# Two rounds of first loads, and the projections of 256 rows ahead of the last two transposes, in a fused SwiGLU feed-forward kernel

## The chip, the cores and the metric

The kernel runs on one core of a Trainium2 chip. The metric is device time in microseconds of one execution; the time before is the median of five runs. One more execution was recorded by the hardware profiler, and all times inside the kernel come from that record.

## The reference

The input x has 2048 rows of 640 columns in bf16 (a leading dimension of 1 is left out here); w_gate and w_up are 640 x 1536, w_down is 1536 x 640.

```python
def reference(x, w_gate, w_up, w_down):
    g = _silu(x @ w_gate)
    u = x @ w_up
    return (g * u) @ w_down
```

## The kernel before

**Tiling.** The rows of x are cut into four blocks of 512 (`sb`), each block into four pieces of 128 rows (`SUB` is 4). The 640 columns are five slices of 128 (`KD`, index `kd`), the 1536 hidden columns are twelve slices of 128 (`KF`, index `fc`). All weights and the whole transposed input `xT` stay in SBUF (the on-chip memory, 128 partitions wide).

**The main loop.** For each block and each `fc`, `proj` issues five matmuls that add up 128 hidden columns x 512 rows of the gate product in a PSUM tile `pg`, and five more for the up product in `pu` (line 133). ScalarE computes Silu of `pg` into `sg` (L170), VectorE multiplies it with `pu` into `aT` (L171). After the twelve `fc` of a block, for each piece of 128 rows, 24 matmuls compute the output (`po_a` of 512 columns at L180, `po_b` of 128 columns at L189), ScalarE copies the result to SBUF, and SyncE (SP) sends it out.

**The start.** TensorE needs x transposed. For the blocks 1 to 3 a transposing DMA does that (L96). For block 0 the four pieces of x are loaded as they are into `x_sb` and TensorE transposes them: `transpose_chunk(c, ...)` issues five transposes (L124) of piece `c` into a PSUM tile `pt`, and a copy takes that to `xT` (L129). The copies are VectorE's, but for three of the five slices of the last piece, which ScalarE takes. Pieces are transposed in the order 0, 2, 1, 3. Ahead of them `warm(N_WARM)` issues 20 matmuls on a tile of ones (L102), which compute nothing that is used, and two more stand between the last transpose and the first projection. The first gate projection is split by rows: 0 to 383, then 384 to 511; the up projection covers all 512.

**The loads.** The first loads go out on two DMA queues, SP's and ScalarE's, each in the order of the code: SP loads the x pieces 0 and 1, ScalarE the pieces 2 and 3 (L73); then both load the first 128 columns of w_gate (SP three of the five slices, ScalarE two), then those of w_up (L86). All further weight chunks go out on SP (L70), gate and up in turn: columns 128 to 383 first, then three chunks of 384 columns each. The framework gives the DMAs eight semaphores in turn, so that the ninth DMA must wait until the DMA that had the first semaphore has landed, the tenth until that of the second has, and so on.

**The order of the work.** The framework orders each engine's instructions and sets the waits. `keep_order`, called at the end of the first step (`sb == 0`, `fc == 0`), holds TensorE and ScalarE to the order in which the code names the instructions. TensorE works in order: an instruction that waits holds up all that stand behind it.

Of the kernel before, what the change touches and what calls it, by code (L numbers as in the profile page):

```python
# [10 lines left out]
def _body(  # L11
# [8 lines left out]
    nc = tc.nc  # L20
    P = nc.NUM_PARTITIONS
# [5 lines left out]
    B, S0, D = x.shape  # L27
    F = w_gate.shape[1]
    S = B * S0
# [3 lines left out]
    KD = D // P  # L33
    KF = F // P
    S_BLK = 512
    NSB = S // S_BLK
    SUB = S_BLK // P
    DA = 512
    N_WARM = 20
    W_CHUNKS = [(0, 1), (1, 3), (3, 6), (6, 9), (9, 12)]  # L40
    assert D % P == 0 and F % P == 0 and S % S_BLK == 0 and D > DA and SUB >= 2

    consts = ctx.enter_context(tc.tile_pool(name="consts", bufs=1))
    work = ctx.enter_context(tc.tile_pool(name="work", bufs=3))
# [8 lines left out]
    wg_sb = consts.tile([P, KD, F], bf16)  # L53
    wu_sb = consts.tile([P, KD, F], bf16)
# [7 lines left out]
    wg_v = w_gate.rearrange("(kd p) f -> p kd f", p=P)  # L62
    wu_v = w_up.rearrange("(kd p) f -> p kd f", p=P)
    wd_v = w_down.rearrange("(kf p) d -> p kf d", p=P)

    def wslice(a, b):
        return slice(a * P, b * P)
# [4 lines left out]
    def load_x(eng, c0, c1):  # L72
        eng.dma_start(out=x_sb[:, c0:c1, :], in_=x_v[:, c0:c1, :])  # L73
# [4 lines left out]

    queues = (nc.sync, nc.scalar)
    halves = ((0, KD // 2 + 1), (KD // 2 + 1, KD))  # L80
    for c in (0, 1):
        for i, eng in enumerate(queues):
            load_x(eng, c + 2 * i, c + 2 * i + 1)
    for dst, src in ((wg_sb, wg_v), (wu_sb, wu_v)):
        for eng, (k0, k1) in zip(queues, halves):
            eng.dma_start(out=dst[:, k0:k1, wslice(0, 1)], in_=src[:, k0:k1, wslice(0, 1)])  # L86
    load_w(nc.sync, wg_sb, wg_v, *W_CHUNKS[1])
# [12 lines left out]
    def warm(n):  # L100
        for _ in range(n):
            nc.tensor.matmul(  # L102
                pw[:, 0:P], lhsT=ones[:], rhs=ones[:], start=True, stop=True
            )

    def keep_order(engine):

        traced = [i for i in nc.cur_bb.bb.instructions if i.engine == engine]
        for a, b in zip(traced, traced[1:]):
            tc.add_manual_dep(  # L110
                b,
                a.name,
                mybir.DependencyInfo(
                    mybir.DependencyClass.NoSync, mybir.DependencyReason.DATA
                ),
                reason="keep_order",
            )

    def transpose_chunk(c, parts):
        c_sl = slice(c * P, (c + 1) * P)  # L120
        for copy, tag, k0, k1 in parts:
            pt = psum.tile([P, k1 - k0, P], bf16, tag=tag, name="pt")
            for kd in range(k0, k1):
                nc.tensor.transpose(  # L124
                    out=pt[:, kd - k0, :],
                    in_=x_sb[:, c, kd * P : (kd + 1) * P],
                    identity=ident[:],
                )
            copy(out=xT[:, k0:k1, c_sl], in_=pt[:])  # L129

    def proj(ps, w_sb, fc, sb, c0, c1):
        for kd in range(KD):
            nc.tensor.matmul(  # L133
                ps[:, c0:c1],
                lhsT=w_sb[:, kd, fc * P : (fc + 1) * P],
                rhs=xT[:, kd, sb * S_BLK + c0 : sb * S_BLK + c1],
                start=(kd == 0),
                stop=(kd == KD - 1),
            )

    for sb in range(NSB):
        s_sl = slice(sb * S_BLK, (sb + 1) * S_BLK)
        for fc in range(KF):
            pg = psum.tile([P, S_BLK], f32, tag="gu", name="pg", bufs=4)
            pu = psum.tile([P, S_BLK], f32, tag="gu", name="pu", bufs=4)
            if sb == 0 and fc == 0:
                h = (SUB - 1) * P
                warm(N_WARM)
                for n, c in enumerate((0, 2, 1)):
                    transpose_chunk(  # L150
                        c, [(nc.vector.tensor_copy, ("po_a", "po_b")[n % 2], 0, KD)]
                    )
                transpose_chunk(
                    SUB - 1,
                    [
                        (nc.vector.tensor_copy, "po_b", 0, 2),
                        (nc.scalar.copy, "po_a", 2, KD),
                    ],
                )
                warm(2)  # L160
                proj(pg, wg_sb, fc, sb, 0, h)
                proj(pg, wg_sb, fc, sb, h, S_BLK)
                proj(pu, wu_sb, fc, sb, 0, S_BLK)
                keep_order(mybir.EngineType.PE)
                keep_order(mybir.EngineType.Activation)
            else:
                proj(pg, wg_sb, fc, sb, 0, S_BLK)
                proj(pu, wu_sb, fc, sb, 0, S_BLK)
            sg = work.tile([P, S_BLK], f32)
            nc.scalar.activation(sg[:], pg[:], ACT.Silu)  # L170
            nc.vector.tensor_tensor(  # L171
                out=aT[:, fc, s_sl], in0=sg[:], in1=pu[:], op=ALU.mult
            )

        for j in range(SUB):
            s0 = sb * S_BLK + j * P
            last = sb == NSB - 1 and j == SUB - 1
            po_a = psum.tile([P, DA], f32, tag="po_a", name="po_a")
            for kf in range(KF):
                nc.tensor.matmul(  # L180
                    po_a[:],
                    lhsT=aT[:, kf, s0 : s0 + P],
                    rhs=wd_sb[:, kf, 0:DA],
                    start=(kf == 0),
                    stop=(kf == KF - 1),
                )
            po_b = psum.tile([P, D - DA], f32, tag="po_b", name="po_b")
            for kf in range(KF):
                nc.tensor.matmul(  # L189
                    po_b[:],  # L190
                    lhsT=aT[:, kf, s0 : s0 + P],
                    rhs=wd_sb[:, kf, DA:D],
                    start=(kf == 0),
                    stop=(kf == KF - 1),
                )
            ot = outp.tile([P, D], bf16)
            nc.scalar.copy(ot[:, 0:DA], po_a[:])  # L197
            if not last:
                nc.scalar.copy(ot[:, DA:D], po_b[:])  # L199
                nc.sync.dma_start(out=out2[s0 : s0 + P, :], in_=ot[:])  # L200
            else:
                nc.sync.dma_start(out=out2[s0 : s0 + P, 0:DA], in_=ot[:, 0:DA])
                nc.vector.tensor_copy(out=ot[:, DA:D], in_=po_b[:])  # L203
                nc.scalar.dma_start(out=out2[s0 : s0 + P, DA:D], in_=ot[:, DA:D])
# [76 lines left out]
def kernel(tc, *args):  # L281
    _body(tc, *args)
    tc.close()
    tc.compile()
    _trim(tc.nc)
# [30 lines left out]
```

## Time and profile before

| | |
|---|---|
| median of five runs | 164.85 us (164.42 to 165.17) |
| profiled execution, its own time | 164.42 us |
| its span, first to last instruction | 163.1 us |
| TensorE busy | 159.3 us, 98% of the span |
| VectorE, ScalarE busy | 34.9 us, 44.0 us |
| DMA | 11.27 MB, nearly all loads in the first fifth of the span |

The profiled execution is the fastest of those shown, and 0.43 us below the median. Its span is 1.3 us shorter than its time; the rest lies around the first and the last instruction. In the profile PE is TensorE's matmuls and PEld its weight loads, which overlap with matmuls; DVE is VectorE, ACT is ScalarE, SPq and ACTq are the issuing of DMAs by SP and ScalarE. A row of a group or of the timeline names the line, the operation, output and input tile, shape and count. The chain of waits is followed back from the last instruction, at each step to whatever released it.

### The profile page before, as it was taken

What the parts mean: (1) busy time and instruction counts of PE and PEld (TensorE: products, weight loads), DVE (VectorE), ACT (ScalarE), POOL (GpSimd) and SP (SyncE); (2) the same over time, 40 slices, a digit from 0 to 9 for tenths busy, and PEclk for the clock granted to TensorE, in tenths of its full rate; (3) what the DMA queues carried; (4) which work ended last, traced back from release to release, by engine and by line L of the source; (5) the groups of instructions that cost most, each with busy time, mean ns of one, the idle gap of its engine ahead of it and who ended that gap; (6) DMA issues with size and microseconds to landing.
All of it is one profiled execution on the core that took longest, in us unless ns stands there. A gap on an engine that the chain in (4) does not pass through costs nothing.

```text
span 163.1 us, 2121 instructions
## 1 busy us (share of the span) xinstructions
PE 159.3 (98%) x894; PEld 80.4 (49%) x911; DVE 34.9 (21%) x54; ACT 44.0 (27%) x82; POOL 0.6 (0%) x6
## 2 busy tenths in 40 slices
PE   9899999999999999999999999999999999999994
PEld 8444444456544444455554444445554444445552
DVE  2322233300022333310002333330001333331000
ACT  3222222123322222222232222222233222222321
POOL 1000000000000000000000000000000000000000
PEclk9999999999999999999999999999999999999999
DMA  7999999911110000001210000001111000000112
GB/s 224 261 334 331 362 202 221 159 40 44 40 40 0 0 4 0 0 2 40 81 43 0 0 2 0 0 4 40 40 40 40 4 0 0 0 0 0 44 47 74
DMA packets 18953, 11.27 MB, mean 69 GB/s; under 512 B 9728, under 2 KB 18944, under 8 KB 18944
## 3 DMA queue, kind: packets, MB, share of 16 engines
q1 hardware_dynamic: 17968, 10.65, 24.1%
q10 hardware_dynamic: 976, 0.49, 1.0%
q8 instruction: 7, 0.11, 0.3%
q14 instruction: 2, 0.02, 0.0%
HBM read 6.55 MB, written 2.62 MB: 56 GB/s over the span
## 4 chain that ended last, share of the span: by engine, by line
PE 94%; DMA 4%; issue 1%; DVE 0%; DVEq 0%
PE pg L133 31%; PE pu L133 31%; PE po_a L180 25%; PE po_b L189 7%; DMA wg_sb<-in_w_gate_dram 3%; DMA x_sb<-in_x_dram 2%; DVE ot L203 0%; DVEq L203 0%
## 5 line engine op out<-in xcount | busy, mean ns | idle before, releaser
L133 PE MATMUL pg<-xT,wg_sb 128*128 128x512 bf16 (+2 forms) x242 | 59.5, 375 | 0.6 <-DMA wg_sb<-in_w_gate_dram 0.3
L133 PE MATMUL pu<-xT,wu_sb 128*128 128x512 bf16 x233 | 59.1, 379 | 0.4
L171 DVE TENSOR_TENSOR aT<-sg,pu 128x512 bf16<-128x512 f32 x48 | 33.0, 687 | 111.0 <-PE pu L133 111.0
L170 ACT ACTIVATE sg<-pg 128x512 f32<-128x512 f32 x48 | 28.7, 597 | 72.7 <-PE pg L133 72.7
L180 PE MATMUL po_a<-wd_sb,aT 128*128 128x512 bf16 x185 | 43.4, 379 | 0.3
L133 PEld LDWEIGHTS <-wg_sb 128*128 128x128 bf16 x245 | 23.6, 98 | 28.2 <-DMA wg_sb<-in_w_gate_dram 1.1
L133 PEld LDWEIGHTS <-wu_sb 128*128 128x128 bf16 x240 | 23.4, 98 | 28.1 <-DMA wu_sb<-in_w_up_dram 0.3
L180 PEld LDWEIGHTS <-aT 128*128 128x128 bf16 x192 | 18.3, 98 | 19.8
L197 ACT CAST ot<-po_a 128x512 bf16<-128x512 f32 x16 | 9.4, 585 | 40.4 <-PE po_a L180 38.0
L189 PEld LDWEIGHTS <-aT 128*128 128x128 bf16 x192 | 12.1, 98 | 3.8
L189 PE MATMUL po_b<-wd_sb,aT 128*128 128x128 bf16 x192 | 13.3, 219 | 0.1
L199 ACT CAST ot<-po_b 128x128 bf16<-128x128 f32 x15 | 4.0, 265 | 1.1
L102 PE MATMUL pw<-ones 128*128 128x128 bf16 x22 | 2.6, 305 | 0.4 <-DVE ones L77 0.4
L203 DVE CAST ot<-po_b 128x128 bf16<-128x128 f32 x1 | 0.3, 291 | 12.3 <-PE po_b L189 12.3
L102 PEld LDWEIGHTS <-ones 128*128 128x128 bf16 x22 | 2.2, 142 | 0.4 <-DVE ones L77 0.4
L129 DVE COPY xT<-pt 128x640 bf16<-128x640 bf16 (+1 forms) x4 | 1.5, 436 | 2.9 <-PE pt L124 2.9
L124 PE MATMUL pt<-ident,x_sb 128*128 128x128 bf16 x20 | 1.8, 255 | 0.0
L88 ACT ACT_TABLE_LOAD x1 | 1.3, 1283 | 2.0 <-issue 2.0
L124 PEld LDWEIGHTS <-x_sb 128*128 128x128 bf16 x20 | 1.6, 121 | 0.2 <-DMA x_sb<-in_x_dram 0.2
L129 ACT COPY xT<-pt 128x384 bf16<-128x384 bf16 x1 | 0.5, 478 | 0.8 <-PE pt L124 0.8
masks.py:199 POOL TENSOR_SCALAR_AFFINE_SELECT ident<-ident 128x128 bf16<-128x128 bf16 x1 | 0.3, 292 | 0.1
L88 ACT ACTIVATE silu_first<-ones 128x1 f32<-128x1 bf16 x1 | 0.2, 202 | 0.0
(6 smaller groups left out, 0.8 us busy)
## 6 DMA issues: line engine op xcount, KB each, us to landing
out_dram<-ot SPq DMA_DIRECT2D x15, 160.0 KB, 1.8
wd_sb<-in_w_down_dram SPq DMA_DIRECT2D x1, 1920.0 KB, 12.6
wg_sb<-in_w_gate_dram SPq DMA_DIRECT2D x3, 480.0 KB, 7.8
wu_sb<-in_w_up_dram SPq DMA_DIRECT2D x3, 480.0 KB, 7.5
x_sb<-in_x_dram SPq DMA_DIRECT2D x2, 160.0 KB, 2.7
x_sb<-in_x_dram ACTq DMA_DIRECT2D x2, 160.0 KB, 2.9
wg_sb<-in_w_gate_dram SPq DMA_DIRECT2D x1, 320.0 KB, 4.4
wu_sb<-in_w_up_dram SPq DMA_DIRECT2D x1, 320.0 KB, 5.0
```

Source lines behind the costliest of these rows:

```text
L88: nc.scalar.activation(silu_first[:], ones[:, 0:1], ACT.Silu)
L102: nc.tensor.matmul(pw[:, 0:P], lhsT=ones[:], rhs=ones[:], start=True, stop=True)
L124: nc.tensor.transpose(out=pt[:, kd - k0, :], in_=x_sb[:, c, kd * P : (kd + 1) * P], identity=ident[:],)
L129: copy(out=xT[:, k0:k1, c_sl], in_=pt[:])
L133: nc.tensor.matmul(ps[:, c0:c1], lhsT=w_sb[:, kd, fc * P : (fc + 1) * P], rhs=xT[:, kd, sb * S_BLK + c0 : sb * S_BLK + c1], start=(kd == 0 ...
L170: nc.scalar.activation(sg[:], pg[:], ACT.Silu)
L171: nc.vector.tensor_tensor(out=aT[:, fc, s_sl], in0=sg[:], in1=pu[:], op=ALU.mult)
L180: nc.tensor.matmul(po_a[:], lhsT=aT[:, kf, s0 : s0 + P], rhs=wd_sb[:, kf, 0:DA], start=(kf == 0), stop=(kf == KF - 1),)
L189: nc.tensor.matmul(po_b[:], lhsT=aT[:, kf, s0 : s0 + P], rhs=wd_sb[:, kf, DA:D], start=(kf == 0), stop=(kf == KF - 1),)
L197: nc.scalar.copy(ot[:, 0:DA], po_a[:])
L199: nc.scalar.copy(ot[:, DA:D], po_b[:])
L203: nc.vector.tensor_copy(out=ot[:, DA:D], in_=po_b[:])
```

## The change

The eight first loads go out in another order. Each queue now has an x piece, its part of the gate columns, an x piece, its part of the up columns. SP has the pieces 0 and 2, ScalarE the pieces 1 and 3.

TensorE's order becomes: 17 warm matmuls; transposes of the pieces 0 and 1; two warm matmuls; the gate projection of rows 0 to 127, then of rows 128 to 255; transposes of the pieces 2 and 3; the up projection of rows 0 to 255; the gate projection of rows 256 to 511; the up projection of rows 256 to 511. The copies are shared out as before.

```diff
-    N_WARM = 20
+    N_WARM = 17
+    N_GAP = 2
...
-    for c in (0, 1):
+    for c, dst, src in ((0, wg_sb, wg_v), (SUB // 2, wu_sb, wu_v)):
         for i, eng in enumerate(queues):
-            load_x(eng, c + 2 * i, c + 2 * i + 1)
-    for dst, src in ((wg_sb, wg_v), (wu_sb, wu_v)):
+            load_x(eng, c + i, c + i + 1)
         for eng, (k0, k1) in zip(queues, halves):
             eng.dma_start(out=dst[:, k0:k1, wslice(0, 1)], in_=src[:, k0:k1, wslice(0, 1)])
...
-                h = (SUB - 1) * P
+                h = SUB // 2 * P
+                dve, act = nc.vector.tensor_copy, nc.scalar.copy
                 warm(N_WARM)
-                for n, c in enumerate((0, 2, 1)):
-                    transpose_chunk(
-                        c, [(nc.vector.tensor_copy, ("po_a", "po_b")[n % 2], 0, KD)]
-                    )
-                transpose_chunk(
-                    SUB - 1,
-                    [
-                        (nc.vector.tensor_copy, "po_b", 0, 2),
-                        (nc.scalar.copy, "po_a", 2, KD),
-                    ],
-                )
-                warm(2)
-                proj(pg, wg_sb, fc, sb, 0, h)
+                transpose_chunk(0, [(dve, "po_a", 0, KD)])
+                transpose_chunk(1, [(dve, "po_b", 0, KD)])
+                warm(N_GAP)
+                proj(pg, wg_sb, fc, sb, 0, P)
+                proj(pg, wg_sb, fc, sb, P, h)
+                transpose_chunk(2, [(dve, "po_a", 0, KD)])
+                transpose_chunk(3, [(dve, "po_b", 0, 2), (act, "po_a", 2, KD)])
+                proj(pu, wu_sb, fc, sb, 0, h)
                 proj(pg, wg_sb, fc, sb, h, S_BLK)
-                proj(pu, wu_sb, fc, sb, 0, S_BLK)
+                proj(pu, wu_sb, fc, sb, h, S_BLK)
```

## Prediction

> **What bounds the kernel now.** I read the page's head first, then the chain of waits over the first 9 us, then the timeline of that stretch, then what the SP queue waits for. The page says that TensorE is the kernel:
>
> ```profile
> span 163.1 us, 2121 instructions
> PE 159.3 (98%) x894; PEld 80.4 (49%) x911; DVE 34.9 (21%) x54; ACT 44.0 (27%) x82; POOL 0.6 (0%) x6
> ```
>
> PE is busy for 98% of the span, and the change leaves everything from the second pair of projections (fc=1) on as it is. So only the moment counts at which PE begins fc=1 and then runs without holes. The chain of waits, cut at 9 us, shows what sets it:
>
> ```profile
> 0.12 2.63 DMA x_sb<-in_x_dram
> 2.77 4.43 DMA wg_sb<-in_w_gate_dram
> 7.24 1.25 PE pg L133 x5
> 8.50 0.65 PE pu L133 x3
> ```
>
> (start, length, what). The chain before 7.24 holds no PE instruction: an x piece that lands at 2.75, a gate chunk (wg_sb columns 128 to 383) that SP issues at 2.77 and that lands at 7.20, then the matmuls of fc=1. The list of SP's own waits has one line that explains the 2.77:
>
> ```profile
> SPq L70 <- DMA x_sb<-in_x_dram: 0.9, 1, 0.9
> ```
>
> SP's first load at L70, the ninth of the program, waits for an x piece, and the chain's 0.12 names it: the first piece on ScalarE's queue (its issues are at 0.1 and 0.6). Last the timeline from 2.3 to 7.3 us (start, length, engine, line, operation; in brackets the idle time before and its releaser):
>
> ```profile
> 2.39 1.05 PEld L124 LDWEIGHTS <-x_sb 128*128 128x128 bf16 x10
> 3.27 1.51 DVE L129 COPY xT<-pt 128x640 bf16<-128x640 bf16 x4 [2.94 <-PE pt L124]
> 3.60 0.56 PEld L124 LDWEIGHTS <-x_sb 128*128 128x128 bf16 x10 [0.17 <-DMA x_sb<-in_x_dram]
> 4.38 0.48 ACT L129 COPY xT<-pt 128x384 bf16<-128x384 bf16 x1 [0.84 <-PE pt L124]
> 4.59 1.13 PEld L133 LDWEIGHTS <-wg_sb 128*128 128x128 bf16 x10 [0.31 <-DMA wg_sb<-in_w_gate_dram]
> 4.64 1.25 PE L133 MATMUL pg<-xT,wg_sb 128*128 128x384 bf16 x10 [0.19 <-DVE xT L129]
> 5.94 1.03 PE L133 MATMUL pu<-xT,wu_sb 128*128 128x512 bf16 x4
> 7.24 0.39 PE L133 MATMUL pg<-xT,wg_sb 128*128 128x512 bf16 x1 [0.27 <-DMA wg_sb<-in_w_gate_dram]
> ```
>
> Three readings. First, ten 128-column operations take 1.05 us before 3.4 and 0.56 us after it: PE's pace doubles there, from 0.105 to 0.056 us each (the windows print a granted clock of 1.00 on both sides, so I go by the paces). Second, pg's matmuls start at 4.64, when the third copy ends and the gate columns have just landed. Third, of pu's five matmuls one record is missing: at the 0.216 us of a 512-column matmul (1.08 for five) the first began at 5.73 and PE was free at 5.73 + 1.08 = 6.81. It then idles 0.43 us for the gate chunk. PE has slack there; the load does not. The next up chunk is as tight: issued at 3.18, 5.0 us to landing, so 8.2, against PE's 7.24 + 1.08 = 8.32.
>
> **The change part by part.** *The loads.* Same eight transfers, same bytes, two queues, four each; only the second and third on each queue change places. Landings, from issue plus time to landing: first x pair 2.3 and 2.75; second x pair 0.5 + 3.1 = 3.6 and 0.6 + 3.2 = 3.8; gate 0.91 + 3.6 = 4.5 and 1.03 + 3.7 = 4.7; up 1.38 + 3.9 = 5.3 and 1.52 + 3.8 = 5.3. What lands third in the new order completes the same bytes as before, so x pieces 2 and 3 at 4.5 and 4.7, and up at 5.3. Gate lands one x pair (1.1 us) earlier at about 3.5; its bounds are 3.1 (0.7 after the first pair, the gap that the up pair shows) and 4.7 (no earlier than now).
>
> *The ninth load.* The first piece on ScalarE's queue is still an x piece issued at 0.1, so SP goes on at 2.77, and the bytes ahead of the gate chunk are the same: 7.20. If the transfers mix better or worse I allow 0.3 either way, about half the spread between the third and the fourth pair; I take 0.
>
> *Warm-up.* Three matmuls fewer are 3 x 0.105 = 0.3 us; they end at 2.2 instead of 2.5. The first transpose waits for its x piece (2.35), so at most 0.1 us comes of it.
>
> *Transposes and projections.* PE executes in order, so I follow it. Transposes of pieces 0 and 1 (10 x 0.105): 2.4 to 3.45, the second piece being there at 2.75. Two warm matmuls: 3.6. The copies keep their places: first 3.27 to 3.75, second to 4.16. Gate columns at 3.5. So pg rows 0 to 127 run 3.8 to 4.1 (5 x 0.056) and rows 128 to 255 run 4.2 to 4.5 after the second copy. Then PE reaches the transposes of piece 2 and has that new wait in front of everything: 4.54 to 4.82, piece 3 to 5.10. VectorE starts a copy 0.27 us after the last transpose starts (4.11 to 4.38 in the ACT row): piece 2's 5.03 to 5.5, piece 3's first part to 5.8 (0.28), ScalarE's part 5.31 to 5.79 (0.48). PE meanwhile waits for the up columns at 5.3 (0.2 us idle), does pu rows 0 to 255 (5 x 0.109, midway between the 128- and the 512-column pace) to 5.85, pg's second half to 6.39, pu's second half to 6.94. So PE is free at 6.94 instead of 6.81. The earlier projections have gained nothing, because the up columns end the wait, and they come last in both orders; what they cost, 0.13 us, is covered by the gate chunk that lands at 7.20. That cover is worth 0.3 us. With gate at 4.7 the same walk ends at 7.6: 0.36 us late. With gate at 3.1 it is still 6.94. I take 6.94.
>
> *Copies, Silu, evictions.* ScalarE's Silu of fc=0 moves from 5.93 to about 6.7; the buffer that it frees is wanted by the third gate projection at 9.41. Nothing waits.
>
> *Sum.* fc=1 begins at 7.24 as before, the up chunk at 8.2 still fits, the 155.9 us that follow are unchanged: span 163.1 us, and the profiled execution 164.42 us (1.3 us around the span). The median of the five runs is 164.85, 0.43 above the profiled one. What fits that spread (0.75 us) is the moment at which PE's pace doubles: each us later costs half a us of PE's work once the slack of 0.43 is gone. With the slow pace to the end of fc=0, PE would be free at about 9.15 before and at 9.05 after (the 0.1 us of the warm-up). So 0 in the runs that the load bounds, -0.1 in those that PE bounds: 164.8.
>
> The page "TensorE: Matmul & The Clock Gate" of the Trainium skill (Part 1) says that the faster clock comes after a busy window of about 3.4 us whose phase runs free of the kernel. The trace has the change 3.0 us after the first matmul (0.39), which doesn't contradict it. The rule speaks against this change: it removes warm-up and puts four holes into that window. By it a window that is missed would cost 3.4 us at half pace, an estimate of up to 1.4 us; by the rows alone I count nothing. "DMA: Bandwidth & Descriptors" (Issuing engines are not separate DMA queues) has both queues interleave on the same 16 engines; the landings in pairs agree, and by it too reordering the queues can't move the last of the eight.
>
> **The rivals.** *No change (my forecast)*: own range 164.5 to 165.2, from the 0.3 us on the gate chunk either way.
>
> *Slower: the holes in PE's work delay the doubling of its pace.* PE now idles 0.2 us before the first transpose, about 0.2 and 0.1 between warm-up and the two pg parts, 0.2 for up; before it has 0.17 and 0.3. Against it: before, the pace doubled in spite of 0.4 us of idleness at the start and 0.17 at the very moment. Price: t us later cost t/2 minus the slack of 0.3; it decides from 0.6 us on. One more wait as long as the first (3.0 us) means 1.2 us at most: 166.0, typically half of that, 165.5. A late gate or up landing (the 0.36 above) would end at 165.2, on the edge of being seen.
>
> *Faster: the loads gain from mixing 256-byte rows of weights with 1280-byte rows of x*, and the gate chunk and the up chunk both land early. For it: the windows show 340 GB/s at 2.4 to 3.4, when x moves, and 193 GB/s from 4.64 to 5.73, so there is room. Against it: that slow stretch belongs to the chunks' own first packets, and SP's issue doesn't move. The bound is PE at 6.94, so 0.3 us, plus the 0.43 by which the median lies above the profiled run if that came from late x pieces, which the new order bears better: 0.3 to 0.7, 164.1 to 164.5.
>
> **How the numbers follow.** No change 0.48, slower 0.29, faster 0.23. A comparison of this kernel can tell about 0.3%, 0.5 us. Most of the forecast's own range lies within that (0.43 of the 0.48, the rest split), most of the slower rival's beyond it (0.27), of the faster one about as well (0.2, its bound being so near): faster 0.22, same 0.48, slower 0.30. The range for 8 in 10 takes in all of the faster rival and the slower one's typical price: 164.1 to 165.8.
>
> **What would show it.** Right: pg of fc=1 at 7.2 to 7.3, released by the gate chunk; SP's first L70 load at about 2.8; PE free by 7.0; an idle gap before pu's first part released by wu_sb. Wrong: the gate chunk landing below 7.0 or above 7.5; ten transposes of pieces 2 and 3 at 0.105 us instead of 0.056; PE going from fc=0 into fc=1 without a gap, later than 7.4; or any hole after 9 us, where I assume none.

## The result, and the profile after

The changed kernel takes 165.27 us (median of 28 runs, 164.81 to 166.49) against 164.67 us for the kernel before (median of 54 runs, 164.23 to 165.49). The ratio is 1.0039, with a 95% interval of 1.0029 to 1.0049: it is slower by 0.64 us, 0.48 to 0.81. Runs that took over 1.5% more than the fastest of their kernel are left out of every ratio but stand in the medians: two of twelve in "PE's order alone", two of twelve in "Rows parted by queue", one of twelve in "Seven first loads", one of the 35 runs of the kernel before that the first four experiments are set against. The profiled execution took 164.75 us, its span is 163.4 us, 0.3 us more than before. It is faster than all 28 runs of the median, so it shows only half of the loss.

The head of its page:

```profile
span 163.4 us, 2135 instructions
...
PE 159.6 (98%) x901; PEld 80.9 (49%) x918; DVE 35.1 (21%) x54; ACT 44.0 (27%) x82; POOL 0.6 (0%) x6
```

The chain of waits of the changed kernel, cut at 12 us (start, length, what):

```profile
...
0.12 2.82 DMA x_sb<-in_x_dram
2.94 0.02 issue
2.96 0.38 SPq L71
3.34 0.04 issue
3.38 5.21 DMA wu_sb<-in_w_up_dram
8.60 0.05 issue
8.64 1.25 PE pu L133 x5
```

It is still a chain of loads, but another load ends it: before, the gate chunk at 7.20 was what PE waited for; now it is the up chunk behind it, which lands at 8.60 instead of 8.21. SP's wait for the first piece on ScalarE's queue is there as before, and ends at 2.94 instead of 2.75, so SP issues the up chunk at 3.38 instead of 3.18: of the 0.39 us by which it lands later, 0.20 us is a later issue. In the kernel before the up chunk was issued and waited for like this:

```profile
3.18 0.53 SPq L70 DMA_DIRECT2D wu_sb<-in_w_up_dram  x1
...
8.26 0.82 PEld L133 LDWEIGHTS <-wu_sb 128*128 128x128 bf16 x5 [0.25 <-DMA wu_sb<-in_w_up_dram]
8.34 1.24 PE L133 MATMUL pu<-xT,wu_sb 128*128 128x512 bf16 x5
```

The weight loads of the changed kernel's profile, transposes and projections, in order of time, and the first matmuls of fc=1 (start, length, engine; in brackets the idle time before and its releaser):

```profile
2.39 1.05 PEld L124 LDWEIGHTS <-x_sb 128*128 128x128 bf16 x10 [0.26 <-DMA x_sb<-in_x_dram]
...
4.96 0.56 PEld L124 LDWEIGHTS <-x_sb 128*128 128x128 bf16 x10 [0.41 <-DMA x_sb<-in_x_dram]
5.61 0.44 PEld L133 LDWEIGHTS <-wu_sb 128*128 128x128 bf16 x5
...
6.63 0.54 PEld L133 LDWEIGHTS <-wu_sb 128*128 128x128 bf16 x5
...
7.50 1.03 PE L133 MATMUL pg<-xT,wg_sb 128*128 128x512 bf16 x4
...
8.64 0.33 PEld L133 LDWEIGHTS <-wu_sb 128*128 128x128 bf16 x3 [0.61 <-DMA wu_sb<-in_w_up_dram]
```

The second ten transposes wait until 4.96 for piece 2. PE is free for fc=1 at 7.28 (the row of fc=1's gate matmuls begins at 7.50 with one record missing, 7.50 - 0.216), where it was 6.81 before. So both terms that I had set to zero or small have moved: the up chunk's landing by 0.39 us and PE by 0.47 us. In this execution the up chunk decides: fc=1's up projection starts at 8.64 instead of 8.34, which is the 0.3 us of the span.

The landing records of the trace show which part of the load is late. Each load has 16 of them. Half of the up chunk's are in at 7.26, 7.21 before; the fifteenth is in at 8.13, 8.19 before; the last at 8.60, 8.21 before. So what was moved is not the bulk of the transfer but its last sixteenth. The same comparison can be made over these two profiles and those of the experiments whose loads go out as here or as before: with the new order of the loads the up chunk landed at 8.15, 8.38, 8.60, 8.80, 8.98, 9.10, 9.14 and 10.07 (eight profiles, middle 8.9); with the old one at 8.08, 8.21, 8.28, 8.28, 8.45 and 8.48 (six profiles, middle 8.3). In the middle of the profiles half of it was in at 7.44 (7.38 with the old order), the fifteenth part at 8.67 (8.11), so the last parts are late not in this profile alone. The later issue accounts for some of it: the issue lay at 3.47 in the middle (3.19 to 3.75) with the new order and at 3.30 (3.18 to 3.63) with the old, and from issue to landing the chunk took 5.3 us against 5.0. The gate chunk's middle is 7.3 with both orders. The last x piece landed at 4.43 once and between 5.10 and 5.59 seven times with the new order, and at 3.80 to 4.20 with the old. The Trainium skill ("DMA: Bandwidth & Descriptors", Why a DMA increments its semaphore by 16 and not by 1) says that a load runs on up to 16 engines that finish on their own, and that only the full 16 mean that all data landed. The sixteen records per load agree with that; who waits for a load waits for its slowest sixteenth (the up chunk's came at 8.60, and PE went on at 8.64).

### The profile page after: what moved, and what is told of

Same layout as the page of the kernel before. It is cut to its first block, busy times and chain, and to the rows that moved or that the text cites. A ratio compares the mean times of both kernels' runs of the same rounds, so it can differ in the third digit from the quotient of the medians.

```text
span 163.4 us, 2135 instructions
## 1 busy us (share of the span) xinstructions
PE 159.6 (98%) x901; PEld 80.9 (49%) x918; DVE 35.1 (21%) x54; ACT 44.0 (27%) x82; POOL 0.6 (0%) x6
## 4 chain that ended last, share of the span: by engine, by line
PE 93%; DMA 5%; issue 1%; SPq 0%; DVE 0%; DVEq 0%
PE pu L133 31%; PE pg L133 30%; PE po_a L176 25%; PE po_b L185 7%; DMA wu_sb<-in_w_up_dram 3%; DMA x_sb<-in_x_dram 2%; SPq L71 0%; DVE ot L199 0%; DVEq L199 0%
## 5 line engine op out<-in xcount | busy, mean ns | idle before, releaser
L133 PE MATMUL pu<-xT,wu_sb 128*128 128x512 bf16 (+1 forms) x241 | 59.6, 375 | 0.3
```

The source lines that it names most:

```text
L133: nc.tensor.matmul(ps[:, c0:c1], lhsT=w_sb[:, kd, fc * P : (fc + 1) * P], rhs=xT[:, kd, sb * S_BLK + c0 : sb * S_BLK + c1], start=(kd == 0 ...
```

## The experiments

All times are set against runs of the kernel before on the same chip; "ratio" is to those. Three theories were on record. The load theory: the new order makes the chunks land late. The PE theory: the last x pieces come late, PE has no slack left. The clock theory: holes in PE's work make the doubling of its pace come later. Five of the versions leave out matmuls or read columns or rows other than they should (PE's work shortened, the two x pieces not waited for, the two without the chunks, the one with neither), so they don't compute the reference and serve to measure only.

### PE's work shortened

```diff
-    def proj(ps, w_sb, fc, sb, c0, c1):
+    def proj(ps, w_sb, fc, sb, c0, c1, KD=KD):
...
-                proj(pu, wu_sb, fc, sb, h, S_BLK)
+                proj(pu, wu_sb, fc, sb, h, S_BLK, 1)
```

The last argument leaves one of five matmuls.

> The changed kernel, but of the last part of the first up projection (rows 256 to 511) four of the five matmuls are left out, so PE has 4 x 0.109 = 0.43 us less work before fc=1 and nothing else differs. PE theory (the last x pieces land at 5.1, PE is free for fc=1 only at 7.28 instead of 6.81, and in the median run later still): the loss of 0.6 us shrinks to 0.2 or less. Load theory (the chunks issued ninth and tenth land late: up at 8.6 instead of 8.2): PE only waits longer, the loss stays above 0.45. Clock theory (the holes delay the doubling of PE's pace, 3.8 instead of 3.4, so PE is late): as the PE theory, 0.2 to 0.4, since work at half pace is taken away.

Ratio 1.0025 (1.0009 to 1.0041), 165.33 us. With 0.43 us less to do, most of the loss is still there. In its profile PE waits 0.44 us for the up chunk, which lands at 8.80. That speaks for the load theory, but doesn't settle it: the interval of the loss goes from 0.15 to 0.67 us, and the PE theory had expected 0.2 or less.

### Seven first loads

```diff
-        for eng, (k0, k1) in zip(queues, halves):
+        parts = halves if dst is wg_sb else ((0, KD),)
+        for eng, (k0, k1) in zip(queues, parts):
```

> The changed kernel, but the first up columns go out as one load on SP instead of two halves on both queues: seven first loads, so the gate chunk is the eighth and doesn't wait for a landing. It should be issued at about 1.9 instead of 2.96 us, the up chunk at 2.95 instead of 3.38. Load theory: both chunks land 0.3 us or more earlier and the loss of 0.6 us goes to 0.2 or below. PE theory: PE is still free only at about 7.3, the loss stays at 0.4 to 0.6. Clock theory: 0.6 stays.

Ratio 1.0028 (1.0010 to 1.0047), 165.24 us. Not what the load theory expected: the gate chunk goes out at 1.91 but lands at 7.45, the up chunk at 8.49, and in this profile the last x piece lands at 5.79 and the first up columns at 6.33, and PE is free only at 8.02. One late load was exchanged for another.

### Twenty warm matmuls in the changed kernel

> The changed kernel with the 20 warm matmuls of before instead of 17, which fills the 0.26 us hole ahead of the first transpose. Clock theory: PE's pace doubles at 3.4 as before and the loss of 0.6 us falls to 0.3 or less. PE theory and load theory: 0.6 as with 17, at most 0.1 more.

(N_WARM from 17 back to 20.) Ratio 1.0033 (1.0010 to 1.0056), 165.23 us. The three matmuls make no difference that these runs can tell. In the profile they don't fill the hole: the first x piece lands at 2.80, and PE still waits 0.40 us for it.

### PE's order alone

```diff
-    for c, dst, src in ((0, wg_sb, wg_v), (SUB // 2, wu_sb, wu_v)):
+    for c in (0, SUB // 2):
         for i, eng in enumerate(queues):
             load_x(eng, c + i, c + i + 1)
+    for dst, src in ((wg_sb, wg_v), (wu_sb, wu_v)):
```

> PE's new order alone: the loads go out in the order of before (two x pieces, gate, up on each queue; SP has pieces 0 and 2, ScalarE 1 and 3). Load theory: chunks land as before, 7.2 and 8.2, no loss beyond 0.1 us unless PE is late. PE theory: pg's first parts wait for gate at 4.6, then the walk runs to 7.4 or 7.6, a loss of 0.2 to 0.4, and the last x pieces, at 3.8, are not to blame. Clock theory: the hole ahead of pg is 1 us long, the pace doubles later still, 0.6 or more.

Ratio 1.0083 (1.0056 to 1.0111): 166.36 us; the runs that enter the ratio lie between 164.64 and 166.96. The profiled execution is the fastest of them; its timeline has the hole:

```profile
2.61 0.97 PEld L125 LDWEIGHTS <-x_sb 128*128 128x128 bf16 x10 [0.49 <-DMA x_sb<-in_x_dram]
...
4.43 0.69 PEld L134 LDWEIGHTS <-wg_sb 128*128 128x128 bf16 x10 [0.74 <-DMA wg_sb<-in_w_gate_dram]
5.08 0.60 PEld L125 LDWEIGHTS <-x_sb 128*128 128x128 bf16 x10
```

Here the pace is already 0.06 us per matmul at 5.08, and the run is as fast as before. The pace doubled at 3.5 us, before the hole of 0.74 us. The median run loses 1.7 us (the ratio says 1.4), and the new load order can't be blamed for that. PE's work from 4.43 to the end of fc=0 is about 3 us at the fast pace and twice that at the slow one, so a late doubling is large enough for it; no execution of this version in which it came late was profiled.

### The last two x pieces not waited for

```diff
-                    in_=x_sb[:, c, kd * P : (kd + 1) * P],
+                    in_=x_sb[:, c % 2, kd * P : (kd + 1) * P],
```

> The changed kernel, but the last two sets of transposes read the x pieces 0 and 1 again instead of 2 and 3, so that PE doesn't wait for the pieces that land at about 5; all loads stay. PE theory (PE is late because the last x pieces land at 4.9 to 5.6 in the four profiles with the new load order): PE is then held by the up columns alone, free at about 7.0, and the loss of 0.6 us falls to 0.3 or less. Load theory (the chunks land late whatever PE does): the loss stays above 0.45. Clock theory: a hole of 0.4 us goes, so the pace doubles earlier in some executions; the median falls and the highest time with it (166.5 to about 166).

Ratio 1.0040 (1.0023 to 1.0057), 165.33 us: nothing gained, which is the load theory's number. The chain of its profile is that of the changed kernel:

```profile
...
0.12 3.12 DMA x_sb<-in_x_dram
...
3.68 5.42 DMA wu_sb<-in_w_up_dram
...
9.15 1.04 PE pu L133 x4
```

Without the wait for pieces 2 and 3, PE still stands in front of the up chunk, here until 9.10.

### The chunks not waited for, in the changed kernel and in the one before

```diff
-                proj(pg, wg_sb, fc, sb, 0, S_BLK)
-                proj(pu, wu_sb, fc, sb, 0, S_BLK)
+                wc = 0 if sb == 0 and fc == 1 else fc
+                proj(pg, wg_sb, wc, sb, 0, S_BLK)
+                proj(pu, wu_sb, wc, sb, 0, S_BLK)
```

> The changed kernel, but fc=1 of the first block uses the gate and up columns of fc=0, which are there, so that PE doesn't wait for the chunks; all loads stay. Load theory: it runs from PE's free moment on, 0.3 us better in the profile, and falls to the time of before or below: 164.7 or less. PE theory: PE itself is late, a loss of 0.3 to 0.6 stays.

> The same edit on the kernel before (fc=1 with the columns of fc=0). The difference to the changed kernel with this edit is what PE's side alone costs. If the slack of 0.43 us that the profile showed is there in most executions: 0.3 to 0.4 us faster than before, about 164.3. If the clock doubles late in the median execution and PE is the bound there: less than 0.2.

Changed kernel: ratio 1.0014 (1.0001 to 1.0027), 164.95 us. Kernel before: 0.9995 (0.9978 to 1.0013), 164.58 us. In the changed kernel the wait for the chunks is worth 0.25%, 0.4 of the 0.64 us (0.15 to 0.7 by the two intervals). In the kernel before it is worth nothing that can be told; a gain of up to 0.36 us lies within the interval. So the slack of 0.43 us can't be there in every execution. In the profiled one it isn't, and its timeline says why:

```profile
2.83 2.05 PEld L124 LDWEIGHTS <-x_sb 128*128 128x128 bf16 x20 [0.39 <-DMA x_sb<-in_x_dram]
...
5.47 1.03 PEld L133 LDWEIGHTS <-wg_sb 128*128 128x128 bf16 x8 [0.17 <-issue]
6.46 0.80 PEld L133 LDWEIGHTS <-wu_sb 128*128 128x128 bf16 x5
7.38 0.96 PEld L133 LDWEIGHTS <-wg_sb 128*128 128x128 bf16 x5
```

All twenty transposes run at 0.105 us; the pace doubles only at about 5.7 us, and the first x piece came at 2.78 instead of 2.35. PE reaches fc=1 at 7.59, not at 6.81, and would not have waited for the gate chunk, which landed at 7.11. Of the four profiles with the load order, the PE order and the 20 first warm matmuls of the kernel before, two have the slack (the kernel before and the one with its short hole filled) and two, with the pace doubling at 5.7 and 6.1, don't (this one and the next).

### Seven first loads in the kernel before

> The kernel before with the first up columns in one load on SP: the gate chunk is the eighth load and waits for no landing, so SP issues it at about 1.9 instead of 2.8 us, the up chunk at 2.8. If the chunks bound the kernel before: 0.2 to 0.4 us faster. If the chunks' early packets delay the pieces that PE needs first, as the same edit did in the changed kernel (last x piece 5.8 instead of 5.1): no gain, or 0.2 slower.

(The edit of the second experiment.) Ratio 1.0006 (0.9993 to 1.0019), 164.75 us: no gain from issuing the chunks earlier, as the last experiment leads one to expect.

### The order of the loads alone

Against the kernel before (the queues' loop as in the change, the order of the transposes as the pieces land):

```diff
-    for c in (0, 1):
+    for c, dst, src in ((0, wg_sb, wg_v), (SUB // 2, wu_sb, wu_v)):
         for i, eng in enumerate(queues):
-            load_x(eng, c + 2 * i, c + 2 * i + 1)
-    for dst, src in ((wg_sb, wg_v), (wu_sb, wu_v)):
+            load_x(eng, c + i, c + i + 1)
...
-                for n, c in enumerate((0, 2, 1)):
+                for n, c in enumerate((0, 1, 2)):
```

> The new order of the loads alone: PE's order is that of before (20 warm matmuls, all transposes, then gate, then up), with the pieces transposed as they land, 0, 1, 2, 3. Load theory (new order: some of the 16 engines fall behind, so the last x pieces land at 5 or later and the up chunk at 8.6 to 9.1 instead of 8.1 to 8.5): PE now needs all pieces before it can project, is free at about 8.2 (5.2 + 0.3 for transposes + 0.5 for copies + 2.2), and loses 0.8 to 1.1 us. If the order of the loads were harmless (x pieces at 4.5, chunks as before): 0.2 to 0.4.

Ratio 1.0117 (1.0080 to 1.0154), 166.87 us, more than expected. The last ten transposes wait 1.78 us for the x piece that lands at 5.25, and the pace doubles only long after this hole:

```profile
5.29 0.98 PEld L124 LDWEIGHTS <-x_sb 128*128 128x128 bf16 x10 [1.78 <-DMA x_sb<-in_x_dram]
...
7.83 0.15 PEld L133 LDWEIGHTS <-wg_sb 128*128 128x128 bf16 x1 [0.17 <-issue]
8.14 0.31 PEld L133 LDWEIGHTS <-wg_sb 128*128 128x128 bf16 x4 [0.17 <-issue]
```

The gate matmuls of 384 rows begin 0.32 us apart until about 8.1, when in the kernel before the pace had doubled at 3.4. So the new PE order does help the new load order; it takes back about two thirds of what that costs (1.17% down to 0.39%).

### Neither x pieces 2 and 3 nor the chunks waited for

> The changed kernel with both edits at once: transposes of pieces 2 and 3 read pieces 0 and 1, and fc=1 uses the columns of fc=0. PE then waits for the first x pieces, the first gate and up columns and nothing else. Load theory: all of the loss that the loads cause is gone, at most 0.1 us over the kernel before with the no-chunk edit (164.58). If PE's order itself or the clock costs something (holes, more instructions): 0.2 or more stays.

Ratio 1.0009 (0.9997 to 1.0022), 164.85 us. With both waits taken away, no loss is left that can be told from noise. Against the kernel before with the no-chunk edit (0.9995) there remains 0.14%, which is not resolved. In its profile the one load that still holds PE is the first up columns, 0.80 us, landing at 6.05 where I had 5.3.

### The hole filled, PE's order with the old loads

Against PE's order alone:

```diff
-    N_WARM = 17
-    N_GAP = 2
+    N_WARM = 20
+    N_GAP = 12
```

> PE's new order with the loads of before, where PE had a hole of 0.8 us ahead of the first gate projection and the median was 166.36 us: 20 warm matmuls instead of 17 and 12 instead of 2 ahead of the projection fill the holes. Clock theory (a hole in the window makes the doubling of PE's pace come a window later): 165.4 or less, although PE has more to do. Without it: 166.4 or above, since ten matmuls more cost up to 0.5 us.

Ratio 1.0024 (1.0011 to 1.0038): 164.92 us, where it was 1.0083 and 166.36 without the filling. Thirteen more matmuls, on a tile of ones, make the kernel faster by 1.0 us by the ratios, 1.4 us by the medians, and the runs from 164.64 to 166.96 draw together to 164.73 to 165.50. That is what the clock theory expected for this order of PE.

```profile
2.45 0.92 PEld L125 LDWEIGHTS <-x_sb 128*128 128x128 bf16 x10
3.33 0.71 PEld L103 LDWEIGHTS <-ones 128*128 128x128 bf16 x12
4.76 0.61 PEld L134 LDWEIGHTS <-wg_sb 128*128 128x128 bf16 x10 [0.72 <-DMA wg_sb<-in_w_gate_dram]
```

In this execution the pace doubles at 3.2 us, so the twelve matmuls take only 0.7 us and a hole of 0.72 us stays ahead of the projection; only the hole ahead of the first transposes is gone. At the slow pace the twelve would take 1.3 us and fill it. Both profiles, with and without the filling, have an early doubling, so that the gain comes by way of the doubling is concluded from the times and not seen in a trace, and which of the two fillings makes it isn't separated.

### Rows parted by queue

```diff
-    for c, dst, src in ((0, wg_sb, wg_v), (SUB // 2, wu_sb, wu_v)):
-        for i, eng in enumerate(queues):
-            load_x(eng, c + i, c + i + 1)
-        for eng, (k0, k1) in zip(queues, halves):
-            eng.dma_start(out=dst[:, k0:k1, wslice(0, 1)], in_=src[:, k0:k1, wslice(0, 1)])
+    load_x(nc.sync, 0, 1)
+    load_x(nc.scalar, 1, 2)
+    load_x(nc.sync, 2, 3)
+    load_w(nc.scalar, wg_sb, wg_v, 0, 1)
+    load_x(nc.sync, 3, 4)
+    load_w(nc.scalar, wu_sb, wu_v, 0, 1)
```

> The changed kernel with the first loads parted by size of rows: SP loads x pieces 0, 2, 3, ScalarE piece 1, then all five slices of the first gate columns, then of the first up columns; six first loads, so both chunks go out without waiting. If the mixing of small and large rows on each queue makes the engines fall behind: x pieces by 4.4, chunks no later than 7.2 and 8.2, 0.3 us faster than the changed kernel or more, perhaps as fast as the kernel before. If not: the chunks crowd out the first up columns, and it is as slow as the changed kernel or 0.3 slower.

Ratio 1.0077 (1.0041 to 1.0114), 166.68 us. It is slower than the changed kernel: the gate columns land at 5.39, PE has a hole of 1.88 us ahead of them. Half of their 16 parts are in at 3.76, the fifteenth at 4.97, the last at 5.39, so here too the last sixteenths fall behind, although small and large rows of the first loads are parted by queue, but for ScalarE's first x piece. Mixed rows within a queue are then not the only way to late parts. Since the chunks also go out earlier here, the run doesn't tell what makes them late.

### The changed kernel filled

> The changed kernel with its holes filled: 20 warm matmuls instead of 17, three instead of two ahead of the first projection, and six more ahead of the transposes of piece 2, where PE waits 0.4 us in the profile. Clock theory (the holes make the doubling of PE's pace come later): the loss of 0.39% falls to 0.2% or less. If the chunks' late landing is the cause: 0.35% to 0.45%, nothing gained.

(20, 3, and `warm(6)` ahead of `transpose_chunk(2, ...)`.) Ratio 1.0062 (1.0041 to 1.0083), 165.61 us. It is about 0.4 us slower than the changed kernel, at the edge of what the two intervals can tell: filling the holes brings at most as much as the added work costs. In its profile the loads happened to be early (x at 4.43, up chunk at 8.38), and yet PE got free only at 8.21:

```profile
4.86 0.69 PEld L102 LDWEIGHTS <-ones 128*128 128x128 bf16 x6
5.50 0.96 PEld L124 LDWEIGHTS <-x_sb 128*128 128x128 bf16 x10
```

From its first matmul to the last transposes PE has no hole: it starts a matmul every 0.107 us from 0.5 us on, and the pace doubles only at 6.2. So a late doubling doesn't need a hole.

### A hole in the kernel before

```diff
-    N_WARM = 20
+    N_WARM = 8
```

> The kernel before with 8 warm matmuls instead of 20: they end at about 1.2 us, and PE then idles 1.2 us until the first x piece lands; nothing else changes, no load, no order. Clock theory: the doubling comes up to a window later, PE is free at up to 9.2 instead of 6.8, the median rises by 0.5 to 1.5 us and the highest time to 166.5 or above. Without it: no difference, since the warm matmuls compute nothing.

Ratio 1.0065 (1.0040 to 1.0090): 165.54 us, up to 166.66. Twelve matmuls that compute nothing, left out of a kernel that otherwise stays as it was, cost 1 us.

```profile
2.31 0.98 PEld L124 LDWEIGHTS <-x_sb 128*128 128x128 bf16 x10 [1.16 <-DMA x_sb<-in_x_dram]
```

The first x piece comes as before, at 2.27; what is missing is PE's activity ahead of it. The profiled execution is the fastest of the eleven (164.65); its pace doubles at 5.5.

### The short hole of the kernel before filled

> The kernel before with six instead of two warm matmuls ahead of the first projection, which fills its hole of 0.3 us there. Clock theory: the hole is short, at most 0.2 us gained in the median; where the pace is still slow the four matmuls cost 0.4 us of PE's time, where it is fast they fit into the hole. Expected between 0.2 us faster and 0.3 us slower; if faster than before beyond the noise, holes of 0.3 us matter.

(`warm(2)` to `warm(6)` ahead of the first projection.) Ratio 1.0007 (0.9994 to 1.0019), 164.64 us: no difference. In its profile the pace doubles at 4.1, and PE still waits for the gate chunk, which lands at 7.44:

```profile
7.49 0.76 PEld L133 LDWEIGHTS <-wg_sb 128*128 128x128 bf16 x5 [0.78 <-DMA wg_sb<-in_w_gate_dram]
```

None of these versions beats the kernel before; the two nearest to it that compute everything (seven loads, short hole filled) can't be told from it.

## Why the prediction was right or wrong

I forecast 164.8 us, no change or a little less; it is 0.6 us slower. The range 164.1 to 165.8 holds the median, the direction doesn't hold. Part of the nearness is the base: I reckoned from 164.85, the median of five runs, and over 54 runs it is 164.67.

**What bounds the kernel.** Right for the profiled execution, wrong as a rule for all of them. "PE has slack there; the load does not" rested on one execution, as fast as the fastest of the five shown, in which the pace doubled at 3.4 us and the first x piece came at 2.35. Leaving out the wait for the chunks in the kernel before gained nothing that can be told (0.9995). Across the seventeen profiles the pace doubles anywhere from 3.2 to 6.7 us, in sixteen of them, and at 8.1 in the one where a hole of 1.78 us goes before it. With a late doubling PE is itself the bound. I had this in the text, half a us per us of delay, and used it only to explain the spread between runs; the sum was still made with a slack of 0.43 and a cover of 0.3, and two of the four profiles of that order have no slack at all.

**The loads.** "What lands third in the new order completes the same bytes as before, so x pieces 2 and 3 at 4.5 and 4.7": they landed at 4.92 and 5.10, and later in six of the seven other profiles. "The bytes ahead of the gate chunk are the same: 7.20", and "the up chunk at 8.2 still fits": gate did land at 7.19, up at 8.60. This is the step that failed most: I took the time when a load's last part lands from the bytes ahead of it, and that moved without them. Counting bytes fits the landing of half of the load, which hardly moved (7.26 against 7.21); a wait goes by the last sixteenth, and in the new order that falls behind. The gate chunk at 7.19 is luck, since it lay between 6.88 and 9.01 in the eight profiles. "SP goes on at 2.77" failed too, by 0.19 us, and with it the issue of the chunks. I allowed 0.3 us on the gate chunk and gave it no sign; the middle of the profiles is 0.6 us, on the up chunk, on the side of the loss. Nor did the last of the eight first loads stay, which I had concluded from the queues' sharing of the engines: it landed at 5.57 instead of 5.35 in the two profiles, at 5.06 to 6.10 against 5.33 to 5.64 in the eight and six. Which of the 16 parts fall behind and why is open: the trace shows no engine for a packet, and the run that parted small rows from large ones had late parts too.

**PE's walk.** The order of the steps and the durations held: 0.55 us for each group of five behind the up columns, nothing gained by the early projections. The walk came out at 7.28 instead of 6.94, because the up columns landed at 5.57 instead of 5.3; the transposes, which began at 4.96 instead of 4.54, were done just ahead of that. The edge that I named (a late gate or up landing, 0.36 us) was nearest to what happened, but I put it at the rim of a rival instead of in the sum.

**The slower rival.** That holes cost time is shown: a hole of 1.2 us made in the kernel before costs 1 us, holes filled in PE's order alone gain 1.0 us by the ratios. But the runs don't show it as the cause here: more warm matmuls in the changed kernel gain nothing that can be told (1.0033) or cost (1.0062). The second of these also gives PE up to 1 us more to do at the slow pace, so it doesn't exclude a gain from the filling that is smaller than this cost; and the interval of the first (1.0010 to 1.0056) doesn't exclude the 0.3 us that the clock theory expected of it. The page on the clock gate ("TensorE: Matmul & The Clock Gate", Part 1), which I weighed and then counted as nothing, says that the window is free of the kernel's phase. The doubling anywhere between 3.2 and 6.7 us, 3.5 us apart, agrees with that, but not with the spread of ±500 ns that the page gives for it. It would have told me not to build a sum on one profile's moment of doubling. **The faster rival** had the sign wrong: in the new order the last sixteenths came later, not earlier. Whether the mixing of row sizes does it is not shown.

**The account.** Of 0.64 us, the wait for the chunks is 0.4 (1.0039 to 1.0014). Taking away the wait for x as well brings it to 1.0009. What is left when neither kernel waits for the chunks (1.0014 against 0.9995, 0.3 us) would be PE's side, but isn't resolved. Taking away the x wait alone brings nothing (1.0040), as the chunk then ends the wait anyway: two late loads stand side by side, and the later one is seen. Each half of the change alone costs more than both together: the new load order 1.17%, PE's new order 0.83%, both 0.39%.

## What to carry to other kernels

A load is waited for until its last sixteenth is in, so moving loads about can cost time although the bytes ahead of the critical load don't change; look at its issue and its last landing records, over several profiles, before calling a transfer unmoved. A slack read from the start of one profile is a slack at one moment of the clock: if PE's pace doubles during the stretch, work the sum for an early and a late doubling. Early work for PE is worth only what its last input allows, and a wait put into the stretch before PE's pace doubles can cost more than its length (PE's order alone: about 0.8 us more of holes in its profile than the kernel before, 1.4 us by the ratio).

## What the runs showed of the hardware that was not expected

Matmuls that compute nothing can gain more than they cost: thirteen of them, up to 13 x 0.105 = 1.4 us of PE's time at the slow pace, made a kernel faster by 1.0 us (1.0083 to 1.0024; 1.4 us between the medians). The moment at which PE's pace doubles moved between 3.2 and 6.7 us from one profile to the next, also between kernels whose first microseconds have the same instructions (3.4 in the kernel before, 5.7 with only fc=1's columns changed, where the first x piece came 0.43 us later), and it came at 6.2 in an execution without a hole. Ten of the seventeen traces hold a record of the granted clock. It begins where the pace doubles, at 3.31 us in the kernel before, at 3.77 in the changed one, at 6.68 with PE's work shortened; nothing is recorded ahead of it, which is why the windows print 1.00 there. It is 160.43 us long in nine of them and 157.01 in the tenth, 3.42 us less, though the spans differ by up to 1.1 us: the granted clock seems to change in steps of 3.4 us whose phase differs from one execution to the next. And the sixteen parts of one load of 320 KB landed as far as 3 us apart (7.08 to 10.07, the up chunk in the changed kernel without the wait for chunks).
